# Longformer attention and a two-layer network on one core: another order of loads, copies and network units

## The chip, the core and the metric

The kernel runs on one core of one Trainium2 chip. The core has five engines that work side by side, each through its own list of instructions: PE (TensorE: matmuls and transposes), DVE (VectorE) and ACT (ScalarE) for elementwise work, POOL (GpSimd), which here issues casting DMAs and makes small copies, and SP (SyncE), which issues plain DMAs. PE writes its results to PSUM, which the kernel uses in eight banks; DVE and ACT read them from there.

The metric is device time in microseconds. Three runs of the kernel before took 411.75, 414.14 and 415.15 us; the median is 414.14.

## The reference

Two parts, one behind the other: attention with a band of 32 positions to each side and 8 global positions, for 8 batches of 8 heads (sequence 576, head size 64), and a network with a hidden layer of 2048 on its 4608 rows of 512.

```python
def _attn_ref(q, k, v, global_idx):
    B, H, S, D = q.shape                          # 8, 8, 576, 64
    scores = 1.0 / np.sqrt(D) * np.matmul(q, k.transpose(0, 1, 3, 2))
    pos = np.arange(S)
    mask = np.abs(pos[:, None] - pos[None, :]) <= 32
    is_global = np.zeros(S, dtype=bool)
    is_global[global_idx] = True
    mask = mask | is_global[:, None] | is_global[None, :]
    scores = np.where(mask, scores, -1000000000.0)
    attn = np.exp(scores - np.max(scores, axis=-1, keepdims=True))
    attn = attn / (np.sum(attn, axis=-1, keepdims=True) + 1e-09)
    return np.matmul(attn, v)

def _moe_ref(x, w_in, w_out):                     # (4608, 512), (512, 2048), (2048, 512)
    h = x @ w_in
    g = h * np.cos(h)
    return g @ w_out

def reference(**kw):
    y = _attn_ref(q, k, v, global_idx)
    x = y.transpose(0, 2, 1, 3).reshape(4608, 512)
    return _moe_ref(x, w_in, w_out)
```

All inputs and the output are float32. The kernel computes in float16 with float32 sums, and checks on the way whether the values allow that; if not, a general path at the end computes everything again.

## The kernel before

**Pairs and stages.** Two heads make a pair; there are 32 pairs, four to a batch. A stage s has two pairs, 2s and 2s + 1, and there are 16 stages. A pair's queries are cut into 11 blocks of 56. For each block a `kw` tile holds 8 global and 120 neighbouring keys and a `qb` tile holds the queries of both heads with the 8 global queries. The steps of a pair are:
- `local_k`, `local_q` and `globals_k`, `globals_q` fill `kw` and `qb`. The local part of pairs 0 to 7 comes from `kn` and `qn`, loaded in rows and turned by PE (`turned`); that of pairs 8 and up from `kT` and `qT`, which a transposing DMA has made, by a copy on DVE (lines 415 and 428). The first 8 columns are copied by POOL from `kgT` and `qgT` (lines 392, 396, 397).
- `scores`: the matmuls `st`, in three groups, an exponential on ACT and a product with the mask on DVE (`pm`).
- `values`: the matmuls `pv` of `pm` with the v rows `vw`, whose last column gives the sums, and the division on DVE (`xn`).
- `turn_x`: PE transposes `xn` (`tx`), and DVE copies it into `xT`, the transposed input of the network. At a batch's last pair POOL copies the eight global rows into their places (line 489).

**The network** takes 512 rows of x, a tile, at a time; there are 9. An input unit (`mlp_in`) makes 128 of the 2048 hidden columns of a tile: four matmuls `ph`, a cosine on ACT, a product on DVE (`g`). An output unit (`mlp_out`) is four matmuls `po`; four output units make 128 rows of the output, which DVE or ACT copies out of PSUM. So there are 144 units of each kind.

**Order.** Everything is written out by hand. The string `FRONT` lists the steps of stages 0 and 1 and the loads beside them. The string `ORDER` lists a stage's steps from stage 2 on, in which a, z are the stage's pairs, c, d those of the next stage, s scores, p values, x `turn_x`, k and q `kw` and `qb`, n the squares of `xn` for the check, 1 an input unit and 2 an output unit. A unit that isn't ready is left out at that place: an input unit needs its tile's x, an output unit all 16 input units of its tile. What then remains is the tail, 32 rounds of one input and one output unit and a last tile of outputs.

**Queues.** POOL issues the loads that change the type: `kn` and `qn` (line 258), `w_in` in four parts (639), `w_out` in one (655), the gathers of the global rows, and `cast_half`, which writes v, k and q in float16 to DRAM (lines 247 and 251), one call for four heads. SP issues what reads these float16 copies, the v rows `vw` (306 to 314, runs of 128 bytes), `vg` and the transposes, and the outputs. A `dma_start` on POOL stands in line with POOL's copies.

**PSUM.** Tag "s" has three banks (scores, turns, `tx`), "h" two (`ph`), "o" one (`po`), and `pv` two.

**The check.** `x_squares` sums the squares of `xn`; `weight_squares` squares a quarter of `w_in` on ACT, and `weight_norms` sums it with four matmuls `pn`; both run in stages 2 to 5. `finish_check` joins the sums on DVE and ends with a matmul `pt` and a flag; it stands in the fifth round of the tail.

## Time and profile before

| | |
|---|---|
| median of three runs | 414.14 us |
| the profiled execution's own time | 415.52 us |
| span of its profile | 413.8 us |
| granted TensorE clock, mean | 0.981 |
| PE busy | 332.7 us (80%), 2,678 instructions |
| PE's weight loads busy | 175.7 us (42%) |
| DVE busy | 269.9 us (65%) |
| ACT busy | 240.1 us (58%) |
| POOL busy | 109.2 us (26%) |
| SP's DMA queue, q1 | 27.89 MB, 54.4% of 16 engines |
| POOL's DMA queue, q0 | 18.75 MB, 44.3% of 16 engines |

PE has most of the busy time, and its transfers of weights run beside its matmuls. The busy shares are means over a front, fourteen stages and a tail, which differ. In the rows of the timeline that follow, the columns are the start and the duration in us, the engine, the line, the operation with what it writes and reads, and the shape; in brackets is the idle time before it and what ended it. In the rows of waits the numbers are the sum of the idle time, how many times, and the longest. In the groups they are busy us and the mean of one in ns, then the idle time before them.

### The profile page before, as it was taken

How to read it: one execution, taken by the hardware profiler on the slowest of the kernel's cores; microseconds unless marked ns; L12 is line 12 of the kernel's file. 1: busy time of each engine (PE TensorE's matmuls, PEld its weight loads, DVE VectorE, ACT ScalarE, POOL GpSimd, SP SyncE). 2: the span in 40 equal slices, each digit the busy share in tenths (PEclk: the TensorE clock that was granted, in tenths of full speed). 3: DMA queues.
4: the chain of work that ended last, by engine and by line, in shares of the span. 5: the costliest groups of instructions: out<-in, count | busy, mean ns of one | idle time of the engine just before them, and what ended most of it. 6: DMA issues, size and time to landing. Idle time of an engine off the chain costs nothing.

```text
span 413.8 us, 7344 instructions
## 1 busy us (share of the span) xinstructions
PE 332.7 (80%) x2678; PEld 175.7 (42%) x2678; DVE 269.9 (65%) x600; ACT 240.1 (58%) x351; POOL 109.2 (26%) x236
## 2 busy tenths in 40 slices
PE   0372218787778889997998899799999997999994
PEld 0162206443334445553554455354555542444441
DVE  7645117677568687887888887978888754434410
ACT  2571017888466767774768486667769662444310
POOL 6582004905740290047006400700310010000000
PEclk9999999989989999998999999999999998999999
DMA  6999999999999799999996999999591000101021
GB/s 88 122 169 198 216 150 85 152 135 121 152 114 166 62 135 157 170 107 168 174 118 113 156 191 96 138 136 148 83 119 53 26 27 27 51 27 51 25 78 57
DMA packets 188504, 47.18 MB, mean 114 GB/s; under 512 B 177005, under 2 KB 183405, under 8 KB 188205
## 3 DMA queue, kind: packets, MB, share of 16 engines
q1 hardware_dynamic: 124509, 27.89, 54.4%
q0 software_dynamic: 63952, 18.75, 44.3%
q8 instruction: 23, 0.38, 0.4%
q14 instruction: 20, 0.16, 0.2%
HBM read 47.73 MB, written 21.23 MB: 167 GB/s over the span
## 4 chain that ended last, share of the span: by engine, by line
PE 60%; DVE 8%; ACT 8%; POOL 7%; SPq 6%; issue 5%; DMA 4%; POOLq 0%; ACTq 0%
PE ph L497 27%; PE po L511 24%; PE pv L458 4%; SPq L314 3%; PE st L446 3%; DMA qn<-in_q_dram 2%; SPq L306 2%; ACT cos L500 2%; DVE o L518 2%; PE tx L481 2%; DVE g L501 2%; ACT sq L530 2%; ACT e L448 2%; POOL q L251 2%; DMA vw<-vg 2%
## 5 line engine op out<-in xcount | busy, mean ns | idle before, releaser
L511 PE MATMUL po<-w_out,g 128*128 128x512 f16 x576 | 145.5, 383 | 8.6 <-DVE o L518 8.6
L497 PE MATMUL ph<-xT,w_in 128*128 128x512 f16 x576 | 142.6, 387 | 6.7 <-DVE g L501 6.5
L500 ACT ACTIVATE cos<-ph,pio 128x512 f16<-128x512 f32 x144 | 97.2, 687 | 76.0 <-PE ph L497 75.7
L501 DVE TENSOR_TENSOR g<-cos,ph 128x512 f16<-128x512 f16 x144 | 96.5, 687 | 61.8 <-ACT cos L500 61.1
L511 PEld LDWEIGHTS <-g 128*128 128x128 f16 x576 | 55.7, 98 | 70.7 <-issue 12.1
L497 PEld LDWEIGHTS <-w_in 128*128 128x128 f16 x576 | 54.2, 99 | 69.1 <-issue 12.4
L448 ACT ACTIVATE e<-st 128x512 f16<-128x512 f32 (+1 forms) x96 | 49.4, 562 | 35.2 <-PE st L446 19.2
L489 POOL COPY xT<-xg 128x4 f16 x64 | 13.4, 210 | 199.0 <-DVE xT L484 195.4
L449 DVE TENSOR_TENSOR pm<-e,mask 128x512 f16<-128x512 f16 (+1 forms) x96 | 37.0, 408 | 27.8 <-ACT e L448 25.9
L446 PE MATMUL st<-qb,kw 128*128 128x128 f16 x352 | 33.6, 237 | 9.5 <-POOL kw L392 6.3
L458 PE MATMUL pv<-vw,pm 128*64 128x65 f16 x704 | 20.7, 207 | 22.9 <-DMA vw<-vg 22.8
L446 PEld LDWEIGHTS <-kw 128*128 128x128 f16 x352 | 26.8, 107 | 24.2 <-POOL kw L392 7.7
L469 DVE TENSOR_TENSOR xn<-pv,r_all 128x768 f16<-128x768 f32 x32 | 30.7, 958 | 1.1
L412 ACT COPY kw<-t 128x1320 f16<-128x1320 f16 x8 | 10.1, 1259 | 35.6 <-PE t L405 35.6
L458 PEld LDWEIGHTS <-pm 128*64 128x64 f16 x704 | 16.7, 120 | 26.9 <-DMA vw<-vg 13.5
L251 POOL DMA_DIRECT2D q<-in_q_dram x12 | 27.2, 2265 | 0.0
L530 ACT ACTIVATE sq<-xn 128x1536 f16<-128x1536 f16 x16 | 23.6, 1475 | 0.0
L415 DVE COPY kw<-kT 128x1320 f16<-128x1320 f16 x24 | 22.3, 929 | 0.0
L428 DVE COPY qb<-qT 64x616 f16<-64x616 f16 x48 | 22.1, 459 | 0.3
L481 PE MATMUL tx<-ident,xn 128*128 128x128 f16 x192 | 17.5, 232 | 5.6 <-DVE xn L469 4.8
L251 POOL DMA_DIRECT2D k<-in_k_dram x12 | 20.7, 1729 | 0.2
L463 DVE TENSOR_REDUCE dg<-pv 8x2 f32<-8x12 f32 x32 | 4.8, 151 | 24.4 <-PE pv L458 21.7
(105 smaller groups left out, 249.6 us busy)
## 6 DMA issues: line engine op xcount, KB each, us to landing
out_dram<-o SPq DMA_DIRECT2D x36, 256.0 KB
vw<-v SPq DMA_DIRECT2D x47, 165.0 KB
v<-in_v_dram POOLq DMA_DIRECT2D x16, 288.0 KB
k<-in_k_dram POOLq DMA_DIRECT2D x12, 288.0 KB
q<-in_q_dram POOLq DMA_DIRECT2D x12, 288.0 KB
vw<-v SPq DMA_DIRECT2D x16, 135.0 KB
w_in<-in_moe_w_in_dram POOLq DMA_DIRECT2D x4, 512.0 KB
w_out<-in_moe_w_out_dram POOLq DMA_DIRECT2D x1, 2048.0 KB
```

Source lines behind the costliest of these rows:

```text
L251: nc.gpsimd.dma_start(dst[s].rearrange("t (h d) -> t h d", h=4), dview(src, base, (D, S), (S * D, 4), (1, D)))
L446: nc.tensor.matmul(st[:, j], kp[:, g0 + j], view(qp[:, g0 + j], (1, P)), start=True, stop=True)
L448: nc.scalar.activation(e[:, :n], st[:, :n], AF.Exp, scale=scale)
L449: nc.vector.tensor_tensor(view(pm[:, g0], (1, n * P)), view(e, (1, n * P)), view(mask[:, g0], (1, n * P)), ALU.mult)
L458: nc.tensor.matmul(pv[r0 : r0 + C, j // 6, c0 : c0 + 65], pm[:, j, h], vp[:, j, h], start=True, stop=True)
L469: nc.vector.tensor_tensor(view(xn, (384, 2), (D, 6), (1, D)), view(pv, (512, 2), (65, 6), (1, D)), view(rp, (6, 2), (1, 6), (0, D)), ALU.mult)
L481: nc.tensor.transpose(tx[:, n], xn[:, n], ident16)
L497: nc.tensor.matmul(ph, w_in16[:, j, f * P : (f + 1) * P], xT[:, j, t * TT : (t + 1) * TT], start=(j == 0), stop=(j == NC - 1))
L500: nc.scalar.activation(cos, ph, AF.Sin, bias=pio2)
L501: nc.vector.tensor_tensor(g16[:, f], cos, ph, ALU.mult)
L511: nc.tensor.matmul(po, g16[:, f, s * P : (s + 1) * P], w_out16[:, f], start=(f == 0), stop=(f == NF - 1))
L530: nc.scalar.activation(sq, view(xn, (1, 2 * BP * P)), AF.Square, accum_out=x_sq[:, s : s + 1])
```

## The change

It moves work and adds one small copy; what is computed stays.

1. **Globals.** `globals_k` and `globals_q` are taken out of the steps k and q. For pairs 8 and up they stand at the start of the stage before theirs; for pairs 0 to 3 before the front's steps; for pairs 4 to 7 in `FRONT` as steps g.
2. **Casts.** All casts from half 4 on go into one function `casts`, called at a new step G, behind the second `values` of a stage. It begins with a copy of one element of `xn` on POOL, `gate`, which waits for that `xn`; behind it on POOL stand v, k and q of one half (in stage 4 of two halves, 6 and 7, and the gathers).
3. **Weights.** `w_out` moves from the end of `FRONT` to the start of stage 2. The four parts of `w_in` stand at other places in `FRONT`.
4. **The check.** The four `weight_squares` and `weight_norms` move from stages 2 to 5 to the tail, three rounds apart. `finish_check` is split: its DVE part stands in round 15 of the tail, the matmul and the flag in round 31 (`raise_flag`).
5. **Order of the units.** `ORDER` and `FRONT` are new, and stage 2 has a string of its own, `THIRD`, without output units. An output unit may now start before its tile's inputs are complete: the n-th four hidden parts need only be seven, in the tail twelve, units past their start. How many output units may be out by a stage is held by `outs_by`: none in stage 2, 4 in stage 3, 8 in stage 4, then 8 more with each stage. An input unit may be at most one tile ahead of the outputs. The tail is one loop over input and output units.
6. **PSUM.** In the front, `turned` uses the two banks of "h" and `turn_x` the one of "o", which the network doesn't use yet.

```diff
-ORDER = "sa0 sa1 sa2 2 2 sz0 2 sz1 2 sz2 pa 1 1 2 xa pz 1 1 2 xz n 1 1 kc qc 2 1 1 kd qd 2"
+ORDER = "sa0 sa1 sa2 2 2 2 sz0 2 sz1 sz2 pa 1 1 2 xa pz G 1 1 2 xz n 1 1 2 kc qc 1 kd qd 2 1"
+THIRD = "sa0 sa1 sa2 sz0 sz1 sz2 1 1 pa 1 1 xa pz G 1 1 kc qc xz 1 1 kd qd 1 n 1"
-FRONT = ("W0 k2 s0.0 s0.1 s0.2 q2 s1.0 s1.1 s1.2 k3 q3 L2 p0 s2.0 s2.1 s2.2 c2 W1 x0 p1 s3.0 s3.1 s3.2 p2 x1 "
-         "k4 q4 L3 v4 v5 W2 W3 c3 p3 x2 k5 q5 I O x3 n0 v6 v7")
+FRONT = ("s0.0 s0.1 s0.2 s1.0 s1.1 s1.2 k2 q2 g4 L2 p0 k3 q3 s2.0 s2.1 s2.2 g5 W0 c2 p1 x0 g6 W1 s3.0 s3.1 s3.2 g7 I "
+         "p2 x1 L3 v4 v5 p3 x2 k4 q4 x3 W2 k5 q5 n0 W3 c3 v6 v7")
...
-        t = ps.tile([P, RW, n], FP16, tag="s", bufs=3)
+        t = ps.tile([P, RW, n], FP16, tag="h" if front[0] else "s", bufs=2 if front[0] else 3)
...
-        tx = ps.tile([P, BP, P], FP16, tag="s", bufs=3)
+        tx = ps.tile([P, BP, P], FP16, tag="o" if front[0] else "s", bufs=1 if front[0] else 3)
...
+        return tot, onesf
+
+    def raise_flag(count):
+        tot, onesf = count
         pt = ps.tile([P, 512], FP32, tag="h", bufs=2)
...
-            if ins_q and ins_q[0][0] < ready[0]:
+            if ins_q and ins_q[0][0] < ready[0] and ins_q[0][0] < outs_q[0][0] + 2:
...
-            if outs_q and (outs_q[0][0] + 1) * NF <= ready[1]:
+            t, u = outs_q[0] if outs_q else (NTT, 0)
+
+            need = min(t * NF + 4 * (u % 4) + 12, NTT * NF) if tail[0] else min(t * NF + 4 * (u % 4) + 7, (t + 1) * NF)
+            if outs_q and need <= ready[1] and (tail[0] or NTT * NF - len(outs_q) < outs_by[0]):
                 mlp_out(*outs_q.pop(0))
...
+        def casts(s):
+
+            nc.gpsimd.tensor_copy(gate, xn_of[s][0:1, 1, 0, 0:1])
+            for n in range(4, 2 * B):
+                if s == (n - 2 if n < 7 else n - 3):
+                    cast_half(n, "vkq")
+            if s == 4:
+                for src, dst in ((k, kg32), (q, qg32), (v, vg32)):
+                    gather(src, dst, 1)
...
-        cast_half(4, "kq")
         for s in range(2, B * NP // 2):
-            if s < B * NP // 2 - 2:
-                cast_half(s + 2, "v")
-            if HY <= s + 3 < B * NP // 2:
-                cast_half(s + 3, "kq")
-            if s == 4:
-                for src, dst in ((k, kg32), (q, qg32), (v, vg32)):
-                    gather(src, dst, 1)
-            for step in ORDER.split():
+            if s == 2:
+                nc.gpsimd.dma_start(w_out16, moe_w_out.rearrange("(c p) n -> p c n", p=P))
+            outs_by[0] = 4 * (s - 2) if s < 5 else 8 * (s - 3)
+            for pr in (2 * s + 2, 2 * s + 3):
+                if 8 <= pr < B * NP:
+                    globals_kq(pr)
+            for step in (THIRD if s == 2 else ORDER).split():
...
                     x_squares(s - 1)
-                    if s < 6:
-                        weight_squares(s - 2)
+                elif step == "G":
+                    casts(s)
...
-            if s < 6:
-                weight_norms(s - 2)
         x_squares(B * NP // 2 - 1)
         tail[0] = True
-        for i in range(2 * NF):
+        for i in range(NTT * NF):
             one()
             two()
-            if i == 4:
-                finish_check()
-        two(NF)
+            if i in (3, 6, 9, 12):
+                weight_norms(i // 3 - 1)
+            if i in (0, 3, 6, 9):
+                weight_squares(i // 3)
+            if i == 14:
+                count = finish_check()
+            if i == 30:
+                raise_flag(count)
```

Three places show how this moves instructions. The first is POOL's list in the front; before, this stands in it (kn and qn are the loads of a half, v a cast, kw and qb the globals' copies of a pair):

```order
L258 DMA kn_86<-in_k_dram 72x4x512
L258 DMA qn_88<-in_q_dram 72x4x512
L247 DMA v_81<-in_v_dram 16x9216
L639 DMA w_in_113<-in_moe_w_in_dram 128x4x512
L392 COPY kw_94<-kgT 128x11x8
L396 COPY qb_98<-qgT 64x11x8
L397 COPY qb_98<-qgT 64x11x8
L258 DMA kn_87<-in_k_dram 72x4x512
L258 DMA qn_89<-in_q_dram 72x4x512
L639 DMA w_in_113<-in_moe_w_in_dram 128x4x512 x2
L247 DMA v_81<-in_v_dram 16x9216
```

Now, from the same loads of kn and qn on:

```order
L260 DMA kn_86<-in_k_dram 72x4x512
L260 DMA qn_88<-in_q_dram 72x4x512
L394 COPY kw_95<-kgT 128x11x8
L398 COPY qb_99<-qgT 64x11x8
L399 COPY qb_99<-qgT 64x11x8
L641 DMA w_in_113<-in_moe_w_in_dram 128x4x512
L249 DMA v_81<-in_v_dram 16x9216
L394 COPY kw_96<-kgT 128x11x8
L398 COPY qb_100<-qgT 64x11x8
L399 COPY qb_100<-qgT 64x11x8
L641 DMA w_in_113<-in_moe_w_in_dram 128x4x512
L394 COPY kw_97<-kgT 128x11x8
```

The globals of pairs 5, 6 and 7 now stand between the loads of the front. They write tiles that pairs 1, 2 and 3 have used, so the loads behind them on POOL come after the scores of those pairs.

The second place is POOL's list in a late stage; before:

```order
L392 COPY kw_94<-kgT 128x11x8
L396 COPY qb_98<-qgT 64x11x8
L397 COPY qb_98<-qgT 64x11x8
L392 COPY kw_95<-kgT 128x11x8
L396 COPY qb_99<-qgT 64x11x8
L397 COPY qb_99<-qgT 64x11x8
L247 DMA v_81<-in_v_dram 16x9216
L251 DMA k_80<-in_k_dram 2304x1x64
L251 DMA q_79<-in_q_dram 2304x1x64
L392 COPY kw_96<-kgT 128x11x8
L396 COPY qb_100<-qgT 64x11x8
L397 COPY qb_100<-qgT 64x11x8
```

Now:

```order
L662 COPY gate<-xn 1x1
L249 DMA v_81<-in_v_dram 16x9216
L253 DMA k_80<-in_k_dram 2304x1x64
L253 DMA q_79<-in_q_dram 2304x1x64
L394 COPY kw_94<-kgT 128x11x8
L398 COPY qb_98<-qgT 64x11x8
L399 COPY qb_98<-qgT 64x11x8
L394 COPY kw_95<-kgT 128x11x8
L398 COPY qb_99<-qgT 64x11x8
L399 COPY qb_99<-qgT 64x11x8
L662 COPY gate<-xn 1x1
L249 DMA v_81<-in_v_dram 16x9216
```

The casts stood at a stage's start, ahead of the globals of the next stage. They now follow the gate in the stage's second half, and the globals stand behind them, at the next stage's start, a stage ahead of their use.

The third place is ACT's list where the tail begins; before (sq is the check's last square of xn, cos an input unit, o a finished output block):

```order
L530 ACTIVATE sq,x_sq<-xn 128x1536
L500 ACTIVATE cos<-ph,pio_71 128x512 x7
L516 COPY o<-po 128x512
L500 ACTIVATE cos<-ph,pio_71 128x512 x8
L516 COPY o<-po 128x512
```

Now, with wsq a square of a quarter of the weights:

```order
L524 ACTIVATE sq,x_sq<-xn 128x1536
L494 ACTIVATE cos<-ph,pio_71 128x512
L531 ACTIVATE wsq<-w_in_113 128x2048
L494 ACTIVATE cos<-ph,pio_71 128x512 x3
L531 ACTIVATE wsq<-w_in_113 128x2048
L494 ACTIVATE cos<-ph,pio_71 128x512 x3
L531 ACTIVATE wsq<-w_in_113 128x2048
L494 ACTIVATE cos<-ph,pio_71 128x512 x3
L531 ACTIVATE wsq<-w_in_113 128x2048
L494 ACTIVATE cos<-ph,pio_71 128x512 x2
L510 COPY o<-po 128x512
```

The four squares now stand between the first input units of the tail, and the first block of outputs that ACT copies stands behind twelve of them.

More of the change, by code (lines that the diff above doesn't have):

```diff
@@ L428, in local_q @@
                 nc.vector.tensor_copy(to, view(qT[pr // 2 % 2][hp, pr % 2], (QB, NB), (1, QB)))
-    def copy_k(pr):
-        globals_k(pr)
-        local_k(pr)
-    def copy_q(pr):
-        globals_q(pr)
-        local_q(pr)
     def scores(pr, g):
@@ L583, in two @@
         for _ in range(n):
-            if outs_q and (outs_q[0][0] + 1) * NF <= ready[1]:
+            t, u = outs_q[0] if outs_q else (NTT, 0)
+            need = min(t * NF + 4 * (u % 4) + 12, NTT * NF) if tail[0] else min(t * NF + 4 * (u % 4) + 7, (t + 1) * NF)
+            if outs_q and need <= ready[1] and (tail[0] or NTT * NF - len(outs_q) < outs_by[0]):
                 mlp_out(*outs_q.pop(0))
+    outs_by = [0]
     ready = [0, 0]
-    tail = [False]
-    STEPS = {"k": copy_k, "q": copy_q, "s": scores, "p": values, "x": turn_x}
+    tail, front = [False], [True]
+    STEPS = {"s": scores, "p": values, "x": turn_x}
     with tc.manual_schedule():
@@ L626 @@
             nc.vector.memset(qb[i], 0.0)
-        for pr in (0, 1):
+        for pr in range(4):
+            if pr > 1:
+                load_v(pr)
             load_vg(pr)
@@ L630 @@
             globals_q(pr)
-        for pr in (2, 3):
-            load_v(pr)
-            load_vg(pr)
         pv = ps.tile([P, 2, 512], FP32, tag="pv", bufs=1)
@@ L652, in load_idx, with globals_kq @@
                 for g in range(G))
-        OTHER = {"L": load_qk, "W": load_w_in, "c": lambda s: cast_half(s, "v"), "v": load_values, "n": x_squares,
-                 "I": load_idx, "O": lambda _: nc.gpsimd.dma_start(w_out16, moe_w_out.rearrange("(c p) n -> p c n", p=P))}
+        def globals_kq(pr):
+            globals_k(pr)
+            globals_q(pr)
+        def casts(s):
[6 more added lines that the diff above has]
+                    gather(src, dst, 1)
+        gate = keep.tile([1, 1], FP16)
+        LOCAL = {"k": local_k, "q": local_q}
+        OTHER = LOCAL | {"g": globals_kq, "L": load_qk, "W": load_w_in, "c": lambda s: cast_half(s, "v"), "v": load_values, "n": x_squares,
+                 "I": load_idx}
         for step in FRONT.split():
@@ L658 @@
             f(*[int(x) for x in (step[1:] or "0").split(".")])
-        ready[0] = 1
+        ready[0], front[0] = 1, False
         for i in range(2):
@@ L681 @@
                     x_squares(s - 1)
-                    if s < 6:
-                        weight_squares(s - 2)
+                elif step == "G":
+                    casts(s)
                 else:
-                    f, pr = STEPS[step[0]], 2 * s + "azcd".index(step[1])
+                    f, pr = (STEPS | LOCAL)[step[0]], 2 * s + "azcd".index(step[1])
                     if pr < B * NP:
@@ L695 @@
                 build_globals(1)
-            if s < 6:
-                weight_norms(s - 2)
         x_squares(B * NP // 2 - 1)
         tail[0] = True
-        for i in range(2 * NF):
+        for i in range(NTT * NF):
             one()
             two()
-            if i == 4:
-                finish_check()
-        two(NF)
+            if i in (3, 6, 9, 12):
[6 more added lines that the diff above has]
+                raise_flag(count)
+        assert not outs_q
     es.close()
```

## The prediction
> **What bounds the kernel now.** I read the page first, for the span and the 40 slices of TensorE (PE) and of the DMA engines.
>
> ```profile
> span 413.8 us, 7344 instructions
> PE   0372218787778889997998899799999997999994
> DMA  6999999999999799999996999999591000101021
> ```
>
> A slice is 10.3 us. PE is near full from about slice 10 on and mostly empty in the first six, while the DMA engines are busy from the second slice to about 300 us. So PE sets the end, and what can be won are its gaps. The waits name them.
>
> ```profile
> PE pv L458 <- DMA vw<-vg: 22.8, 3, 13.0
> PE po L511 <- DVE o L518: 8.6, 12, 1.4
> PE st L446 <- POOL kw L392: 6.3, 3, 2.2
> PE pt L567 <- DVE onesf L565: 2.7, 1, 2.7
> ```
>
> PE waits 22.8 us for v rows, 8.6 us for an output bank to be copied out (0.7 us in each of twelve stages), 6.3 us for POOL and 2.7 us in the tail. The timeline of PE's rows gives the milestones.
>
> ```profile
> 48.30 0.26 PE L458 MATMUL pv<-vw,pm 128*64 128x65 f16 x1 [13.00 <-DMA vw<-vg]
> 61.09 1.14 PE L458 MATMUL pv<-vw,pm 128*64 128x65 f16 x22 [9.07 <-DMA vw<-vg]
> 65.65 0.63 PE L446 MATMUL st<-qb,kw 128*128 128x128 f16 x4
> 84.20 0.61 PE L446 MATMUL st<-qb,kw 128*128 128x128 f16 x8
> 103.16 0.78 PE L446 MATMUL st<-qb,kw 128*128 128x128 f16 x11
> 128.15 0.78 PE L446 MATMUL st<-qb,kw 128*128 128x128 f16 x11
> 149.58 0.78 PE L446 MATMUL st<-qb,kw 128*128 128x128 f16 x11
> 167.32 0.78 PE L446 MATMUL st<-qb,kw 128*128 128x128 f16 x11
> 335.04 1.03 PE L497 MATMUL ph<-xT,w_in 128*128 128x512 f16 x4
> ```
>
> The rows at 48.30 and 61.09 are the products of pairs 2 and 3 with their v rows. The front ends at 65.65, where stage 2 starts; stages 3 to 6 start at 84.20, 103.16, 128.15 and 149.58. A stage that nothing disturbs takes 167.32 - 149.58 = 17.74 us. The tail begins at about 335.0 and lasts 78.8 us.
>
> **The front: the loads that leave the way of the v rows.** Here are the queues by window. First 30 to 35 us (q0 is POOL's queue, q1 SP's, which loads vw; packets, then MB), then q1 alone in 60 to 65 us, then both in 232 to 236 us, a time of casts.
>
> ```profile
> q0 software_dynamic: 690, 0.89, 102.0%
> q1 hardware_dynamic: 633, 0.08, 21.2%
> ...
> q1 hardware_dynamic: 2864, 0.36, 101.6%
> ...
> q0 software_dynamic: 2459, 0.48, 138.2%
> q1 hardware_dynamic: 1957, 0.25, 78.9%
> ```
>
> ```profile
> 25.37 4.61 SPq L309 DMA_DIRECT2D vw<-v  x2
> 29.84 1.54 POOL L639 DMA_DIRECT2D w_in<-in_moe_w_in_dram  x2
> 38.32 1.20 POOL L655 DMA_DIRECT2D w_out<-in_moe_w_out_dram  x1 [5.09 <-issue]
> ...
> vw<-v SPq DMA_DIRECT2D x47, 165.0 KB
> w_in<-in_moe_w_in_dram POOLq DMA_DIRECT2D x4, 512.0 KB
> w_out<-in_moe_w_out_dram POOLq DMA_DIRECT2D x1, 2048.0 KB
> kn<-in_k_dram POOLq DMA_DIRECT2D x4, 288.0 KB
> ```
>
> Beside weights SP's loads get 633 / 5 = 127 packets per us; alone 573. A load of 165 KB in runs of 128 B is 1,320 packets, and pairs 2 and 3 need four, with their small vg rows about 5,500. They are issued from 25 us and end at 61. Between 21 and 40 us POOL issues four w_in loads, two kn/qn sets (0.59 MB each), two v casts and w_out: 2.1 + 1.2 + 0.6 + 2.1 = 6.0 MB.
>
> In the change, what is queued on POOL before 40 us is one kn/qn set, two w_in loads and one v cast, 1.9 MB: the globals of later pairs, which wait for a pair's scores, stand between them, and w_out, the other two w_in loads and the last v cast come behind the eight xT copies of x3. At 0.89 / 5 = 0.18 MB per us these 1.9 MB take 10.5 us. In that time q1 moves 1,330 packets; the other 4,200 take 7.3 us alone. So pair 3's v rows land near 25 + 10.5 + 7.3 = 43 instead of 61, and with the 4.6 us from 61.09 to 65.65 stage 2 starts near 48: **-18 us**. The extra PSUM tags ("h" for the turns, "o" for tx) only allow this: I find no wait of the front on a bank above 1 us, so by themselves 0 to -1.
>
> Then the bill. The 3.4 MB held back (two w_in, a v cast, w_out) are issued at about 50, after x3 and the xT copies, and take 3.4 / 0.18 = 19 us, to 69. Behind them on SP's queue stand vw of pairs 6 and 7, on POOL's the gated casts of half 4. From the v cast's landing near 58 to 69 q1 moves 11 x 127 = 1,400 packets, and the other 4,100 go at 1957 / 4 = 489 per us, to 77. Stage 2 loses a weight square and its four matmuls (1.9 us of ACT, 0.9 of PE, rows below) from the 18.55 between 65.65 and 84.20: 17, so stage 3 starts at 65 and would want pair 7 nine us later, at 74. It waits 3; its first output unit also waits for w_out, about 2 more. Stage 4 starts near 87 (before 103.16), and stage 5, 24.99 us later in the original, here some 22 later: four output units fewer and no norm, but the casts of halves 6 and 7 and six gathers now follow one another on POOL, and the DVE copies of kw and qb fall among them (below), 2 to 4 us. **Stage 5 starts near 109 instead of 128.15: -19.** Bounds: 98, if the held-back loads hide altogether (48 + 17 + 16 + 17); 121, if each of stages 3 to 5 waits another 4 us.
>
> At this point a rule of the Trainium skill speaks against the change. "DMA: Bandwidth & Descriptors", section "Queues, rings and completion order", says that a DMA engine serves its queues in turn, a packet from each. By this rule w_out's large rows slow SP's small ones wherever w_out stands. The trace agrees: 690 packets against 633.
>
> **Eleven full stages, 5 to 15.** They take 335.04 - 128.15 = 206.9 us, 18.8 each. The row of PE's wait on POOL, and what led to it, in one such stage and, last two rows, in the next, clean one:
>
> ```profile
> 224.75 2.84 DVE L415 COPY kw<-kT 128x1320 f16<-128x1320 f16 x1
> 225.05 2.19 POOL L251 DMA_DIRECT2D q<-in_q_dram  x1
> 228.55 0.38 PE L446 MATMUL st<-qb,kw 128*128 128x128 f16 x4 [2.07 <-POOL kw L392]
> ...
> 244.71 0.53 DVE L415 COPY kw<-kT 128x1320 f16<-128x1320 f16 x1
> 248.50 1.02 PE L511 MATMUL po<-w_out,g 128*128 128x512 f16 x4 [0.66 <-DVE o L518]
> ```
>
> Two things end here. POOL's k and q casts, queued ahead of the next stage's globals, hold PE, and while they issue, DVE's copy of kw takes 2.84 us instead of 0.53. In the change the globals of the next stage stand at a stage's start and the casts behind the gate, after the stage's last xn. A gate costs POOL a copy of one element, which I put at 0.3 us (no row of before shows one); behind it wait the casts, the xT copies and the next globals, all wanted 5 us later or more. DVE's order after xn is two g, the xT copies, two g, then kw and qb. I estimate that work at 5 us (a g like a cos, 0.69 in the rows of the tail, and PE's units between) and the casts at 4 (2.19 for q in the row, k no longer), so the copies mostly come after them. And the new ORDER puts scores between the last matmul of an output block and the first of the next, so the 0.66 us goes. A stage is then 17.74 - 0.66 = 17.1; I take 17.4, for the order brings PE close to DVE's pace. 11 x 17.4 = 191.4: **-15.5**. Bounds: 17.1 (-18.8) and 18.0 (-8.9).
>
> Can the DMA engines follow? In the clean stage they did, with the same casts, v rows and outputs, in 17.74 us; 0.3 less is asked of them.
>
> **The tail.** What leaves it and what comes:
>
> ```profile
> 342.81 1.03 PE L511 MATMUL po<-w_out,g 128*128 128x512 f16 x4
> 346.66 1.39 PE L497 MATMUL ph<-xT,w_in 128*128 128x512 f16 x4
> 350.95 1.03 PE L511 MATMUL po<-w_out,g 128*128 128x512 f16 x4
> 394.11 13.98 PE L511 MATMUL po<-w_out,g 128*128 128x512 f16 x64
> ...
> L537 ACT ACTIVATE wsq<-w_in 128x2048 f16<-128x2048 f16 x4 | 7.6, 1898 | 0.0
> L543 PE MATMUL pn<-wsq,ones 128*128 128x512 f16 x16 | 4.1, 378 | 0.5 <-DVE g L501 0.5
> L500 ACT ACTIVATE cos<-ph,pio 128x512 f16<-128x512 f32 x144 | 97.2, 687 | 76.0 <-PE ph L497 75.7
> ```
>
> A unit of four matmuls takes 13.98 / 16 = 0.87 us. From 342.81 to 350.95 four units run in 8.14 us instead of 3.5: the check's wait and the slow matmuls behind it cost 4.7. With its flag matmul sixteen steps after its DVE part, this is hidden behind output units: -4.7. The sixteen norm matmuls come in: +3.5, four units' time, all PE (their row has 4.1 beside other waits). The new rule of two() lets input units run ahead alone, eight or so; with two banks each waits for the cos (0.69) and the g (put at the same) of the one before the last, and 0.3 for handing over, an estimate: (0.87 + 0.69 + 0.69 + 0.3) / 2 = 1.27 instead of 0.87, +3.2. Of the four 1.9 us squares on ACT some 2 us show. Sum **+4** (from -1, all hidden, to +8, every square shown).
>
> **Sum.** 109 + 191.4 + 78.8 + 4 = 383 of span. The profiled execution's 415.52 stands 1.4 above the median 414.14, which is within 0.4 of the span 413.8; I go by the median: **384**.
>
> **Rivals.** *The loads are only postponed.* The v rows of pairs 6 to 11 each meet w_out or the late casts; stages 3 to 5 keep their old length, stage 5 starts at 121: 396. For: 127 packets per us beside weights. Against: w_out lasts about 12 us of a 17 us stage.
> *The bill never shows.* Stage 5 at 98, the rest as summed: 373. For: q1 has a stage's lead.
> *Slower: the lock of the casts.* If DVE reaches kw and qb before the q cast is issued, each of stages 3 to 15 pays as at 224.75, where the two copies of the casts cost 2.3 us, and with four copies and POOL's xT copies up to twice that, 4.5. Stage length 17.4 + 4.5 = 21.9: 11 x 21.9 = 241, stage 5 at 118: 118 + 241 + 82.8 = 442. At 2.3 it is 109 + 217 + 83 = 409. It turns slower than before from about 2.7 us per stage. For: casts were in the way of three stages and are now in all. Against: the 5 us of DVE work ahead. The Trainium skill, "SBUF — State Buffer", section "SBUF: two separate sides", has this as an exclusive lock between GpSimd and certain DVE operations; the row at 224.75 agrees.
> *It does not do what it says.* Another queue holds the front (the v casts, half 1), gain 5, and stages 18.3: 407 to 412.
>
> **Chances.** Forecast 0.50; postponed 0.20; bill never shown 0.16; does not do it 0.07; lock 0.07. Range 370 to 404: it takes in the forecast, most of the hidden bill and the postponed loads, some 0.82. The three runs of before spread from 411.75 to 415.15, so 1% is about what can be told. Faster by over 1% (under 410): 0.88; within 1%: 0.06; slower: 0.06.
>
> **What would show it.** Pair 3's product near 43 and stage 2's first scores near 48; q1's packets per us above 400 before 45; no PE wait on POOL kw and none on o of 0.66; L415 at 0.53 from stage 5 on; stage starts 17.4 apart; a pt matmul without wait; a tail of about 83 us. I am wrong if pv waits for vw again in stages 2 and 3 for over 8 us, or if L415 stays long in every stage.

## The result, and the profile after

The changed kernel takes 396.06 us (median of four runs, 395.26 to 397.13); the kernel before took 414.38 beside it (411.75 to 415.15). The ratio is 0.957, with a 95% interval from 0.952 to 0.962. The forecast was 384, with a range of 370 to 404: faster as forecast, by 18 us where 30 were forecast. Of the kernels with the early cast and with the old order, further down, one execution each, the profiled one, ran in a slower state of the chip (394.99 and 407.23 us): it is left out of their times (with it the medians are 390.21 and 400.55), and its rows are read for what lies between them, not for where they stand.

The profiled execution took 397.13 us. Its page, with the 40 slices of PE, of PE's granted clock and of the DMA engines:

```profile
span 395.4 us, 7373 instructions
PE   0272179576778889899999999999999979999993
PEclk9997558969999999999999999999999999999999
DMA  6989979999999999999999999999990000010121
```

A slice is 9.9 us now. The front is still empty, and the DMA engines are still full from the second slice to about 300 us. New in the record is a clock of 0.5 in the fifth and sixth slice. The rows don't show PE slower there than before, though the record of the kernel before has 1.00: six transposes `tx` take 0.82 us at 62.17 before the change and 0.82 at 50.51 after it, against 0.50 to 0.51 later on in both. The waits of PE after the change (sum, times, longest):

```profile
PE pv L452 <- issue: 10.3, 2, 9.4
PE pv L452 <- DMA vw<-vg: 8.5, 4, 5.1
...
PE pv L452 <- DMA vw<-v: 4.2, 2, 3.0
...
PE po L505 <- DMA w_out<-in_moe_w_out_dram: 3.6, 1, 3.6
...
PE po L505 <- DVE o L512: 1.3, 1, 1.3
...
PE st L440 <- POOL qb L399: 1.0, 1, 1.0
```

The wait for v rows is still 23 us (10.3 + 8.5 + 4.2; the 9.4 called issue stands ahead of pair 2's product, which reads v rows). There is a new one for w_out, 3.6. The wait for POOL fell from 6.3 to 1.0 and the one for o from 8.6 to 1.3. The milestones in PE's timeline:

```profile
49.81 0.77 PE L452 MATMUL pv<-vw,pm 128*64 128x65 f16 x21 [1.20 <-DMA vw<-v]
...
55.47 1.35 PE L440 MATMUL st<-qb,kw 128*128 128x128 f16 x11
...
74.98 0.78 PE L440 MATMUL st<-qb,kw 128*128 128x128 f16 x11
79.32 1.49 PE L505 MATMUL po<-w_out,g 128*128 128x512 f16 x4 [3.57 <-DMA w_out<-in_moe_w_out_dram]
...
83.50 1.02 PE L452 MATMUL pv<-vw,pm 128*64 128x65 f16 x22 [1.52 <-DMA vw<-vg]
...
91.61 0.76 PE L452 MATMUL pv<-vw,pm 128*64 128x65 f16 x22 [3.03 <-DMA vw<-v]
...
99.68 0.77 PE L440 MATMUL st<-qb,kw 128*128 128x128 f16 x11 [0.95 <-POOL xT L483]
...
118.22 0.77 PE L440 MATMUL st<-qb,kw 128*128 128x128 f16 x11 [0.76 <-issue]
...
140.05 0.81 PE L440 MATMUL st<-qb,kw 128*128 128x128 f16 x11
...
192.29 0.78 PE L440 MATMUL st<-qb,kw 128*128 128x128 f16 x11
...
209.20 0.78 PE L440 MATMUL st<-qb,kw 128*128 128x128 f16 x11
...
309.84 1.89 PE L491 MATMUL ph<-xT,w_in 128*128 128x512 f16 x8
```

| | before | after | difference |
|---|---|---|---|
| stage 2 starts | 65.65 | 55.47 | -10.2 |
| stage 3 starts | 84.20 | 74.98 | -9.2 |
| stage 4 starts | 103.16 | 99.68 | -3.5 |
| stage 5 starts | 128.15 | 118.22 | -9.9 |
| the tail starts | 335.04 | 309.84 | -25.2 |
| the span ends | 413.8 | 395.4 | -18.4 |

So the front's 10 us are mostly gone at stage 4: stage 3 takes 24.7 us, with 8.1 us of waits for loads. Stage 4, 24.99 before, takes 18.54; what shortened it is not taken apart here. The eleven stages from 5 on take 191.6 instead of 206.9, and a clean one 209.20 - 192.29 = 16.91 instead of 17.74. The tail takes 85.6 instead of 78.8.

DVE's copies of kw, by group; before the change, then after it:

```profile
L415 DVE COPY kw<-kT 128x1320 f16<-128x1320 f16 x24 | 22.3, 929 | 0.0
```

```profile
L417 DVE COPY kw<-kT 128x1320 f16<-128x1320 f16 x24 | 13.3, 556 | 0.0
```

No copy takes 2.8 us any more; the longest is 0.96.

### The profile page after: what moved, and what is told of

The parts are those of the page before. It is cut to its first block, busy times and chain, and to the rows that moved or that the text cites. A ratio compares the mean times of both kernels' runs of the same rounds, so it can differ in the third digit from the quotient of the medians.

```text
span 395.4 us, 7373 instructions
## 1 busy us (share of the span) xinstructions
PE 328.3 (83%) x2678; PEld 174.7 (44%) x2678; DVE 260.6 (66%) x600; ACT 238.8 (60%) x351; POOL 114.8 (29%) x250
## 4 chain that ended last, share of the span: by engine, by line
PE 67%; DMA 10%; DVE 8%; ACT 5%; issue 3%; SPq 3%; another core or an unknown queue 1%; POOL 0%; ACTq 0%; DVEq 0%
PE po L505 28%; PE ph L491 27%; DMA q<-in_q_dram 4%; PE st L440 4%; PE pv L452 4%; DMA vw<-vg 3%; DMA vw<-v 3%; DVE g L495 2%; PE tx L475 2%; SPq L308 2%; ACT cos L494 2%; DVE xn L463 1%; PE t L407 1%; ACT sq L524 1%
## 5 line engine op out<-in xcount | busy, mean ns | idle before, releaser
L505 PE MATMUL po<-w_out,g 128*128 128x512 f16 x576 | 140.4, 380 | 5.0 <-DMA w_out<-in_moe_w_out_dram 3.6
L442 ACT ACTIVATE e<-st 128x512 f16<-128x512 f32 (+1 forms) x96 | 47.6, 561 | 14.3 <-PE st L440 9.3
L662 POOL COPY gate<-xn 1x1 f16<-1x1 f16 x14 | 2.5, 182 | 143.3 <-DVE xn L463 143.3
L452 PE MATMUL pv<-vw,pm 128*64 128x65 f16 x704 | 20.6, 204 | 23.1 <-issue 10.3
L440 PE MATMUL st<-qb,kw 128*128 128x128 f16 x352 | 30.8, 238 | 4.2 <-ACT e L442 1.5
L483 POOL COPY xT<-xg 128x4 f16 x64 | 20.5, 320 | 22.0 <-DVE xT L478 18.6
L510 ACT COPY o<-po 128x512 f32<-128x512 f32 x18 | 10.5, 586 | 22.4 <-PE po L505 21.9
L512 DVE COPY o<-po 128x512 f32<-128x512 f32 x18 | 12.3, 685 | 12.1 <-PE po L505 12.0
```

Source lines behind the costliest of these rows:

```text
L440: nc.tensor.matmul(st[:, j], kp[:, g0 + j], view(qp[:, g0 + j], (1, P)), start=True, stop=True)
L442: nc.scalar.activation(e[:, :n], st[:, :n], AF.Exp, scale=scale)
L452: nc.tensor.matmul(pv[r0 : r0 + C, j // 6, c0 : c0 + 65], pm[:, j, h], vp[:, j, h], start=True, stop=True)
L505: nc.tensor.matmul(po, g16[:, f, s * P : (s + 1) * P], w_out16[:, f], start=(f == 0), stop=(f == NF - 1))
```

## Experiments

The theory at this point: the late stages gain by the gate and the early globals; the front's loads are only postponed, since the DMA queues are full up to stage 4. The rival: the order of the loads makes the front's gain, and the order of the units that of the late stages. Each kernel but the last two is the changed one with one edit, and the kernel before, run beside them, took 412.1 to 413.3 us. The changed kernel was not run again beside them, so the ratios to the kernel before (0.957 for the changed kernel) tell more than differences in us; 0.01 is 4 us.

### The loads of the front

All loads back at the places of the kernel before:

```diff
-FRONT = ("s0.0 ... g5 W0 c2 p1 x0 g6 W1 s3.0 s3.1 s3.2 g7 I "
-         "p2 x1 L3 v4 v5 p3 x2 k4 q4 x3 W2 k5 q5 n0 W3 c3 v6 v7")
+FRONT = ("W0 s0.0 ... g5 c2 W1 p1 x0 g6 s3.0 s3.1 s3.2 g7 I "
+         "p2 x1 L3 v4 v5 W2 W3 c3 p3 x2 k4 q4 O x3 k5 q5 n0 v6 v7")
...
-            if s == 2:
-                nc.gpsimd.dma_start(w_out16, ...)
```

> The changed kernel with all five loads of the front's POOL list (four parts of w_in, the v cast of half 3, w_out) put back where they stood among the steps of the kernel before; the globals stay where the change put them. Theory 1, as predicted: these bytes take the DMA engines from pair 3's v rows. Then pair 3's product, at 49.8 in the changed kernel and 61.1 in the one before, lies at 56 to 60, stage 2 starts at 61 to 65 instead of 55.5, stage 3 has no wait for v rows and w_out, and the time is 396 to 402. Theory 2, the front moves a fixed number of packets and any order gives the same start of stage 4: stage 4 starts at 95 to 100 and the time is 391 to 396, like the runs with w_out (394.1) or the v cast (390.2) moved alone.

394.07 us, ratio 0.955 (0.948 to 0.962): no slower than the changed kernel. Its rows of PE:

```profile
55.06 0.23 PE L452 MATMUL pv<-vw,pm 128*64 128x65 f16 x1 [11.32 <-DMA vw<-vg]
56.19 0.81 PE L452 MATMUL pv<-vw,pm 128*64 128x65 f16 x21 [0.89 <-DMA vw<-vg]
...
98.38 0.77 PE L440 MATMUL st<-qb,kw 128*128 128x128 f16 x11 [0.98 <-POOL xT L483]
```

Both theories are right on what they describe. The mechanism of the front is there: with the weights ahead of them, pair 3's rows come at 56.19 instead of 49.81, and stage 2 starts at 61.88. But stage 3 then waits for no load, and stage 4 starts at 98.4, as in the changed kernel (99.7). **All in all the new order of the loads moves the wait from the front to stage 3 and brings nothing by stage 4.** But this run moves the v cast of half 3 along with the weights, and that cast is worth some 5 us when it alone stands early (below): what the late weights bring, the late v cast takes back. With w_out alone back in the front it is the same:

```diff
-         "p2 x1 L3 v4 v5 p3 x2 k4 q4 x3 W2 k5 q5 n0 W3 c3 v6 v7")
+         "p2 x1 L3 v4 v5 p3 x2 k4 q4 O x3 W2 k5 q5 n0 W3 c3 v6 v7")
```

> The changed kernel with one edit: the load of w_out is issued ahead of the xT turn of pair 3, near 40 us, as before the change, instead of at the start of stage 2 (60.3). Theory 1, taking w_out out of the way of pair 3's v rows is what brought the front's gain: these rows, which land at 49.8, land near 56, stage 2 starts near 61 instead of 55.5; the wait for w_out in stage 3 (3.6 us) goes; the time is 398 to 401. Theory 2, w_out's place only chooses which wait shows: stage 4 starts within 1 us of 99.7 and the time is 395 to 397.

394.07 us, ratio 0.956 (0.950 to 0.962). Pair 3's rows come at 52.2 instead of the 56 expected, stage 2 starts at 57.9, and stage 4 at 94.8, 5 us earlier than theory 2 had it; the time is the same all the same, for stages 5 and 6 then take 20.5 and 20.7 us. The Trainium skill ("DMA: Bandwidth & Descriptors", section "Queues, rings and completion order") has it that a DMA engine serves its queues in turn, a packet from each. What the prediction drew from that, that w_out slows the small rows wherever it stands, fits these two runs: pair 3's rows come 2.4 us later with w_out ahead of them, and 6.4 with all the weights.

To test the bound itself, half of the weights' bytes are left out:

```diff
-        x3 W2 k5 q5 n0 W3 c3 v6 v7
+        x3 k5 q5 n0 c3 v6 v7
...
-            nc.tensor.matmul(ph, w_in16[:, j, f * P : (f + 1) * P], ...
+            nc.tensor.matmul(ph, w_in16[:, j, f % 8 * P : (f % 8 + 1) * P], ...
...
-            nc.tensor.matmul(po, g16[...], w_out16[:, f], ...
+            nc.tensor.matmul(po, g16[...], w_out16[:, f % 8], ...
...
-                nc.gpsimd.dma_start(w_out16, ...)
+                nc.gpsimd.dma_start(w_out16[:, 0:8], ...)
```

> The changed kernel with half of the weights' bytes: two of the four parts of w_in are loaded and 1 MB of w_out, and the units use the loaded half twice, so the output is another; every instruction of PE, DVE and ACT stays. Theory 1, up to stage 4 the kernel is bound by what the two DMA queues can move, so that an order of the loads shifts waits and not their sum: 2 MB less at the 0.19 MB per us that POOL's queue moves there is 10 us less in the way, the waits for w_out and v rows in stage 3 (8 us) go, stage 4 starts near 91 instead of 99.7, and the time is 387 to 390. Theory 2, the v rows alone and the engines set it: stage 4 starts at 97 or later, the time is 393 or more.

389.66 us, ratio 0.944 (0.939 to 0.948); the output is another. Stage 4's first scores in this run:

```profile
93.72 0.77 PE L440 MATMUL st<-qb,kw 128*128 128x128 f16 x11 [0.95 <-POOL xT L483]
```

6.0 us earlier and 6.4 us in all: stage 3 waits for bytes. Theory 1 has the time right and the start too early: it is less than the 10 us that the bytes take, for stage 3 then takes 18.0 us, near its own work. The sum of the bytes isn't the whole bound either: with all of them, and w_out early, stage 4 starts at 94.8.

Which bytes can come earlier at no cost? In the changed kernel SP's queue all but stops from 55 to 60 us, and from 60 to 70 it has no row. Its packets from 55 to 60, then a window of PE (length, busy time, clock, share of the DMA engines, GB/s), then the rows of POOL's timeline, then of SP's:

```profile
q1 hardware_dynamic: 59, 0.01, 1.5%
```

```profile
52.00:60.00 8.00, 5.83 (x80) 0.50 0.46 34
```

```profile
55.51 2.05 POOL L483 COPY xT<-xg 128x4 f16 x8 [15.52 <-DVE xT L478]
57.67 1.55 POOL L641 DMA_DIRECT2D w_in<-in_moe_w_in_dram  x2
59.20 0.55 POOL L249 DMA_DIRECT2D v<-in_v_dram  x1
```

```profile
52.62 1.49 SPq L316 DMA_DIRECT2D vw<-vg  x2
67.82 3.89 SPq L311 DMA_DIRECT2D vw<-v  x2
```

The v cast of half 3, from which pairs 6 and 7 are loaded, stands on POOL behind the xT copies, which wait 15.5 us for pair 3. SP can go on only at 67.82. POOL's other loads stand there too, so from 52 to 60 us the DMA engines move little at all: 34 GB/s, and 197 in the 8 us behind it. So this cast alone was moved ahead:

```diff
-         "p2 x1 L3 v4 v5 p3 x2 k4 q4 x3 W2 k5 q5 n0 W3 c3 v6 v7")
+         "p2 x1 L3 c3 v4 v5 p3 x2 k4 q4 x3 W2 k5 q5 n0 W3 v6 v7")
```

> The changed kernel (396.1 us, 0.957 of before) with one edit: the v cast of half 3 (pairs 6 and 7) stands ahead of the v loads of pair 4 in the front's string, so POOL issues it near 40 us instead of 59.2. In the changed kernel SP's queue has 59 packets between 55 and 60 us and none from 60 to 70. Theory 1, the late cast leaves that queue idle and so makes the rows of pairs 6 and 7 late: those rows land before 72, the two waits of PE for v rows in stage 3 (1.5 and 3.0 us) go, stage 2 starts at most 2 us later since the cast now shares with pair 3's rows, and the time falls by 3 to 5 us, to about 392. Theory 2, the bytes are only postponed and some load is late whatever the order: pair 3's rows land 3 us later, or w_out does, and the time stays within 1 us of 396.

388.93 us, ratio 0.944 (0.938 to 0.950): **5 us faster than the changed kernel by the ratios, 7 by the times**, a little more than theory 1 said. Stage 3 takes 95.27 - 78.42 = 16.9 us instead of 24.7 and waits for no v rows (2.6 us for w_out stay), and SP's queue moves 2,609 packets from 56 to 60 us. In its profiled execution stage 2 starts at 58.80, 3.3 later, where theory 1 allowed 2. The loss was a queue that stood idle for one cast. It also shows what the late weights are worth: with the v cast early, the kernel takes 388.93 us with the weights late and 394.07 with them at their old places (the v cast's own place differs a little between the two). So moving the weights was worth some 5 us, and the v cast that was moved with them hid it.

### The late stages: gate and globals

The casts at the start of the stage, ahead of the globals, without the gate:

```diff
         for s in range(2, B * NP // 2):
...
+            casts(s)
             for pr in (2 * s + 2, 2 * s + 3):
                 if 8 <= pr < B * NP:
                     globals_kq(pr)
...
         def casts(s):
-            nc.gpsimd.tensor_copy(gate, xn_of[s][0:1, 1, 0, 0:1])
...
                 elif step == "G":
-                    casts(s)
+                    pass
```

> The changed kernel with the casts at the start of the stage, ahead of the globals, without the gate; order, loads and tail stay. Theory 1, what held PE before the change was that the globals stood behind the casts in the stage that needs them; as they now stand a stage ahead, the place of the casts does not matter: late stages stay at 16.9 to 17.2, the time at 395 to 399. Theory 2, the gate keeps the casts off DVE's copies and products: DVE rows beside a cast take 2 to 3 us more, three or more stages grow by 2 us as at 224.75 in the kernel before, the time is 402 or more.

413.60 us, ratio 1.002 (0.999 to 1.006). **Without the gate the whole gain is gone**, and stages 8 to 11 take 18.3 to 20.1 us. Theory 2 has the time; its mechanism is only a part. DVE's 24 copies of kw take 22.3 us in all again. What stands on DVE, POOL and PE around one late stage:

```profile
217.41 0.53 DVE L417 COPY kw<-kT 128x1320 f16<-128x1320 f16 x1
219.42 2.15 DVE L417 COPY kw<-kT 128x1320 f16<-128x1320 f16 x1
...
238.38 0.95 DVE L430 COPY qb<-qT 64x616 f16<-64x616 f16 x2 [3.38 <-DMA qT<-q]
```

```profile
217.96 1.64 POOL L253 DMA_DIRECT2D k<-in_k_dram  x1
219.03 2.18 POOL L253 DMA_DIRECT2D q<-in_q_dram  x1
...
223.40 1.64 POOL L253 DMA_DIRECT2D k<-in_k_dram  x1
224.47 2.18 POOL L253 DMA_DIRECT2D q<-in_q_dram  x1
```

```profile
219.34 0.78 PE L440 MATMUL st<-qb,kw 128*128 128x128 f16 x11
...
239.43 0.80 PE L440 MATMUL st<-qb,kw 128*128 128x128 f16 x6 [2.87 <-issue]
```

Two things come back. POOL, held by nothing, issues a cast in the last microseconds of a stage, where DVE copies kw: five of the 24 copies take 2.15 to 3.35 us. This is what the prediction called the lock. The Trainium skill, "SBUF — State Buffer", section "SBUF: two separate sides", calls the ports that GpSimd and certain DVE operations share an exclusive lock; these rows agree on the block, and show it on the side of DVE while POOL issues. And the casts of two stages go out within 10 us of one another, at 218 and 223; the transposes and v rows behind them come late: DVE waits 3.38 us for qT and PE 2.87 for DVE. With the gate the k casts stand 16.92 us apart, one stage, at 204.04 and 220.96. PE's waits of this kind past the front, and a longer one for o:

```profile
PE st L440 <- issue: 7.5, 5, 2.9
...
PE po L505 <- DVE o L512: 4.1, 1, 4.1
```

That is 11.6 us, 9.5 more than in the changed kernel, of the 17.5 in all; the rest is not taken apart further. **The late stages pay for the second thing, not for the lock**: the copy of 2.15 us at 219.42 costs PE 0.1 us, and the stage loses its 3 us ahead of 239.43, to qT. The lock costs in stage 4, where the wait for o of 4.1 us stands behind the copy of 3.35. That it is the pairing of the casts that makes the transposes late is read from these rows; no run tests it alone.

The other half: the globals back in the steps k and q, with the gate left.

```diff
-            for pr in (2 * s + 2, 2 * s + 3):
-                if 8 <= pr < B * NP:
-                    globals_kq(pr)
...
-        LOCAL = {"k": local_k, "q": local_q}
+        LOCAL = {"k": both_k, "q": both_q}    # globals, from pair 8 on, and the local part
```

> The changed kernel with the globals of pairs 8 and up back in the steps that fill kw and qb, behind the gated casts on POOL; all else stays. Theory 1, moving the globals a stage ahead is half of the late stages' gain: POOL ends the casts some 4 us behind the gate and then copies, PE waits for kw or qb by about 2 us in most stages, the time is 410 or more. Theory 2, the gate alone does it, since the casts end before the copies are wanted: late stages stay at 16.9 to 17.3, the time at 396 to 400.

416.87 us, ratio 1.010 (1.006 to 1.013). All of the gain is gone here too. PE's waits, then the row of the longest and what POOL waited for ahead of it:

```profile
PE st L440 <- POOL qb L399: 25.5, 6, 17.4
```

```profile
137.34 0.26 POOL L399 COPY qb<-qgT 64x88 f16<-64x88 f16 x1 [5.93 <-DMA vg<-in_v_dram,gidx_rows]
```

```profile
137.66 1.33 PE L440 MATMUL st<-qb,kw 128*128 128x128 f16 x11 [17.38 <-POOL qb L399]
```

17.4 of the 25.5 us stand ahead of stage 5: in stage 4 two halves of casts and six gathers lie between the gate and the globals. From there on it is 1.1 to 1.2 us ahead of stages 8, 10 and 12, where the xT copies stand in between too. So theory 1 is right in direction and result, but not by 2 us in most stages. The DVE copies stay short (13.5 us in all), as the gate has it. A gate puts the casts right ahead of the next stage, so the globals must no longer stand behind them. But nearly all of the price is the double cast and the gathers of stage 4: from stage 5 to the end this run takes 277.9 us and the changed kernel 277.1. What late globals cost with the gathers elsewhere was not run.

### Order, gathers, norms, banks

The old order of steps from stage 3 on:

```diff
-ORDER = "sa0 sa1 sa2 2 2 2 sz0 2 sz1 sz2 pa 1 1 2 xa pz G 1 1 2 xz n 1 1 2 kc qc 1 kd qd 2 1"
+ORDER = "sa0 sa1 sa2 2 2 sz0 2 sz1 2 sz2 pa 1 1 2 xa pz G 1 1 2 xz n 1 1 kc qc 2 1 1 kd qd 2"
```

> The changed kernel with the old order of steps from stage 3 on (the step G, the casts, put behind the second pair's values); globals, casts, loads and tail stay as changed. A late stage takes 16.92 us in the changed kernel and took 17.74 before, undisturbed. Theory 1, the order of the units brought this 0.8: a late stage takes 17.7 again and the time is 0.8 x 12 = 10 us longer, 405 to 406. Theory 2, it came from the globals and casts: a late stage stays below 17.1, the time at 396 to 398.

398.54 us, ratio 0.968 (0.960 to 0.976). Two starts of stages in it:

```profile
199.43 0.78 PE L440 MATMUL st<-qb,kw 128*128 128x128 f16 x11
...
216.84 0.78 PE L440 MATMUL st<-qb,kw 128*128 128x128 f16 x11
```

A clean stage takes 17.41 us, between the two theories: of the 0.83 between 17.74 and 16.91 the order brings 0.50. Stages 8 to 14 are clean in both kernels, so this makes 3.5 us; the time is 2.5 us longer by the medians and 4.6 by the ratios.

The gathers at the start of stage 3:

```diff
-            if s == 4:
-                for src, dst in ((k, kg32), (q, qg32), (v, vg32)):
-                    gather(src, dst, 1)
...
+            if s == 3:
+                for src, dst in ((k, kg32), (q, qg32), (v, vg32)):
+                    gather(src, dst, 1)
             for step in (THIRD if s == 2 else ORDER).split():
```

> The changed kernel with the six gathers of the second half's global rows issued at the start of stage 3, behind its globals, instead of behind the two halves of casts in stage 4. Stage 5 takes 21.8 us in the changed kernel, where a late stage takes 16.9. Theory 1, the gathers on POOL and in the DMA queue beside the double cast cause most of this: stage 5 takes 18 to 19 us, the time is 393. Theory 2, it is the build of the global columns and the double cast: stage 5 stays above 21 and the time within 1 us of 396.

394.20 us, ratio 0.952 (0.945 to 0.959), which can't be told from the changed kernel. Stage 5 takes 18.9 us, as theory 1 has it; but it takes 18.9 too in the runs with the old loads, with the old banks and with half of the weights, where the gathers stay. What made it 21.8 in the changed kernel's profile is left open.

The weight squares and norms back in stages 2 to 5:

```diff
                 elif step == "n":
                     x_squares(s - 1)
+                    if s < 6:
+                        weight_squares(s - 2)
...
+            if s < 6:
+                weight_norms(s - 2)
...
-            if i in (3, 6, 9, 12):
-                weight_norms(i // 3 - 1)
-            if i in (0, 3, 6, 9):
-                weight_squares(i // 3)
```

> The changed kernel with the four weight squares and norms back in stages 2 to 5. They cost 1.9 us of ACT and 0.9 us of PE each. Theory 1, as the prediction has it, in the tail they are paid for, in stages 2 to 5 they partly lie beside waits for DMA: the tail falls from 85.6 by 5 to 6 us, stages 2 to 5 grow by 1 to 4 in all, the time is 392 to 395. Theory 2, stages 2 to 5 pay in full, 1.9 us of ACT each: the time is 396 to 399.

392.56 us, ratio 0.949 (0.943 to 0.955): theory 1. The tail takes 390.9 - 312.9 = 78.0 instead of 85.6, and stages 2 to 5 together 89.1 instead of 84.6. The stages grow by 4.5, a little more than theory 1 allowed, and the tail falls by 7.6. So this part of the change costs some 3 us, at the edge of what can be told, since the intervals of the two ratios meet.

The banks of the front:

```diff
-        t = ps.tile([P, RW, n], FP16, tag="h" if front[0] else "s", bufs=2 if front[0] else 3)
+        t = ps.tile([P, RW, n], FP16, tag="s", bufs=3)
...
-        tx = ps.tile([P, BP, P], FP16, tag="o" if front[0] else "s", bufs=1 if front[0] else 3)
+        tx = ps.tile([P, BP, P], FP16, tag="s", bufs=3)
```

> The changed kernel with the turns and the tx of the front back in the three banks of tag s. Theory 1, as predicted, the banks only allow and bring nothing by themselves: 396 within 1 us, since the front waits for loads. Theory 2, with the loads moved the banks have become a wait: pair 3's scores come later, stage 2 starts 2 us or more after 55.5, the time is 398 or more.

395.56 us, ratio 0.958 (0.953 to 0.964): no effect, as predicted. Its stage 4 starts at 97.8 and its stage 6 at 135.2, against 99.7 and 140.1: so much do executions with the same loads differ there.

### A faster version, and the clock

Three edits together: the early v cast, the gathers in stage 3 (as above), the norms in stages 3 to 6 (`3 <= s < 7` and `s - 3` in the diff of the norms).

> The changed kernel with the v cast of half 3 early (390.2 alone), the gathers at the start of stage 3 (394.2 alone), and the weight squares and norms in stages 3 to 6 instead of the tail (392.6 alone in stages 2 to 5). If the gains lie in different places they add: 4 to 6 by the cast, 1 to 2 by the gathers, 3 to 4 by the norms, so 385 to 388. If the DMA queues still set stages 3 to 6, the gathers and the norms' place give nothing beside the cast: 389 to 391.

389.50 us, ratio 0.942 (0.937 to 0.946): it beats both kernels, and the early cast alone does so by as much (388.93). The gains do not add. The tail falls to 78.5, but stages 3 to 7, freed of waits by the cast, now show each square: input units wait for g by up to 2.35 us behind a square of ACT.

To this, matmuls that nothing reads were added where PE waits for v rows in the front:

```diff
-         "p2 x1 L3 c3 v4 v5 p3 x2 ...
+         "d30 p2 x1 L3 c3 v4 v5 d12 p3 x2 ...
...
+        def busy(n):
+            t = ps.tile([P, 512], FP32, tag="o", bufs=1, name="idle")
+            for _ in range(n):
+                nc.tensor.matmul(t, ident16, view(mask[:, 0], (1, 512)), start=True, stop=True)
```

> The kernel of the three moves with 42 matmuls of 512 columns that nothing reads, 30 ahead of pair 2's product and 12 ahead of pair 3's, where PE waits for v rows. In the changed kernel the granted clock is 0.50 from 36 to 60 us and a group of 11 score matmuls takes 1.35 us instead of 0.78 there. Theory 1, the clock falls because PE idles and the front pays for it: kept busy, PE runs at full clock from 45 to 63, stage 2 starts 2 to 3 us earlier, and the time falls by 1 to 3 us against the three moves. Theory 2, loads set the front and the slow matmuls lie beside them: stage 2 starts up to 2 us earlier and stage 4 does not, the time is the same within 1 us.

389.48 us, ratio 0.943 (0.938 to 0.948): the same time. Windows of PE in this run (length, PE's busy time, its clock, the DMA share, GB/s):

```profile
48.00:50.00 2.00, 0.75 (x24) 1.00 1.29 102
...
52.00:54.00 2.00, 1.85 (x35) 0.50 1.46 109
```

The clock stays at 1.00 up to pair 3's product, and stage 2 starts 2.0 us earlier than without, stage 4 1.6, which is less than such starts differ between executions. In the time nothing is left of it, as theory 2 has it. Theory 1 is not refuted in full: it wanted full clock up to 63, and from 52 to 60 us, where stage 2 begins, the clock was 0.50 all the same.

## Why the prediction was right or wrong

The range held the time, the direction was right, and the forecast was 12 us too low. By its own sum, of the span: 109 + 191.4 + 82.8 = 383 was forecast, and 118.2 + 191.6 + 85.6 = 395.4 measured.

- **The front, "-18": measured -10, and gone again by stage 4.** The step that failed is "stage 2 starts near 48". "What is queued on POOL before 40 us is one kn/qn set" was wrong: a second one was issued at 38.5, and is in neither the 1.9 nor the 3.4 MB of the sum. Beside them SP's queue did better than the 127 packets per us taken, 221 and 262 per us in the windows of 30 to 35 and 40 to 45 us:

```profile
q1 hardware_dynamic: 1107, 0.14, 27.3%
...
q1 hardware_dynamic: 1312, 0.16, 37.5%
```

  Pair 3's product came at 49.8 instead of 43, and from there to stage 2 it took 5.7 instead of 4.6 us. Its sign, "above 400 before 45", failed too. The run with the old loads shows that the cause named was real (56.2 against 49.8); its price was paid back in stage 3, by waits for w_out (3.6) and for the v rows behind the cast that was moved with the weights (4.5).
- **The bill, "stage 5 near 109": 118.2.** This is the term that was mis-sized, by 9. Stage 2 started 7.5 us late, and the forecast let stage 3 wait 3 + 2 us; it waited 8.1. The reason was seen only in part: the v cast of half 3 was put among the loads held back, but not that SP's queue would stand idle for some 12 us for it. The rival "the loads are only postponed" (396) names this mechanism and the time; its stage 5 at 121 counts 4 us of waits in stage 5 itself, which lie behind that start; without them it is 117, near the 118.2. "The bill never shows" is refuted.
- **Eleven stages, "17.4": 191.6 against 191.4, by offsetting errors.** A clean stage takes 16.91, below the bound of 17.1; stages 5 (21.8) and 7 (18.4) take the rest back, so that the sum holds is luck. That "two things end here" was right: the wait on POOL's globals and that on o are gone, and the copy of kw is short. The mis-sized term is the wait on o, "0.66". In the kernel before, four scores take 0.23 us from start to start with the bank free (151.92) and 1.05 with the wait (153.01):

```profile
151.92 0.39 PE L446 MATMUL st<-qb,kw 128*128 128x128 f16 x4
152.15 1.03 PE L511 MATMUL po<-w_out,g 128*128 128x512 f16 x4
153.01 0.39 PE L446 MATMUL st<-qb,kw 128*128 128x128 f16 x4
154.06 1.02 PE L511 MATMUL po<-w_out,g 128*128 128x512 f16 x4 [0.66 <-DVE o L518]
```

  So it cost 0.82, and 17.74 - 0.82 = 16.92. The price of the parts was not seen: all of the gain is gone when the gate or the early globals are taken away.
- **The lock, as a rival: refuted for this kernel, by a hair.** "DVE's order after xn" kept the copies behind the casts: none takes longer than 0.96 us. But the "5 us" of DVE work are 4.0 in a late stage (xn ends at 203.25, kw begins at 207.28), and the casts behind the gate, itself 0.18 us, end at 207.30. Without the gate some copies are blocked, as the rival says, but the late stages lose their time to late transposes; that 413.6 lies in the rival's range, 409 to 442, is chance.
- **The tail, "+4": +6.8.** The flag's wait fell from 2.7 to 0.5 us, as said. The windows show 132 and 193 matmuls of units in the tail instead of 128 and 189, another 1.7 us, which the sum had left out. With the norms' 3.5, 4.2 us of waits for g (1.35, 1.55, 0.64 and 0.63), where 3.2 + 2 were forecast, and 4.7 less for the check, 4.7 of the 6.8 are named. The two units come out of stage 15, which takes 16.05 us.
- **The banks, "0 to -1"**: 0, within what can be told.

Where the 18 us lie, by the starts of the stages: 3.5 by stage 4, 6.5 in stage 4, 15.3 in stages 5 to 15, and the tail gives 6.8 back. What each part is worth when it alone is undone: 17 to 19 us for the gate, some 21 for the early globals, most of it in stage 4, and 2.5 to 4.6 for the order of the units; the norms in the tail cost some 3, the late v cast 5 to 7. These don't add up, since they depend on one another.

## What to carry to other kernels

Where transfers bound a stretch, moving several out of the way at once can move the wait only; look for the queue that then stands idle, and leave early what it waits for. An instruction that issues transfers in an in-order queue is worth placing by what stands behind it as much as by what it collides with: hold it by a gate, and take what is needed soon out from behind it. Undo each part alone before crediting it: parts that need one another each seem to be worth the whole gain, and two that work against each other can seem to be worth nothing. Then look in the rows whether the time was lost where the theory said.

## What the hardware showed

- The clock of PE fell to 0.50 without one long idle time: in the last run it was 1.00 from 38 to 50 us and 0.50 from 52 to 60, and ahead of that PE idled 1.13, 0.33 and 1.02 us between 47.8 and 52.2 us, the last as it fell. In the changed kernel it was 0.50 from 36 to 60, and a group of 11 score matmuls took 1.35 us instead of 0.78. A group at 33.94 in the kernel before took 1.35 us too, where the record shows 1.00; so in the front the lengths of the rows tell more than the record. What the half clock costs here is not shown.
- A DVE copy of kw (128x1320) that meets the issue of k and q casts on POOL can take 2.15 to 3.35 us instead of 0.53, four to six times as long, while the cast's own issue rows keep their 1.64 and 2.18 us. Not each one does: copies of qb (64x616) beside the k cast keep 0.45 to 0.47, and a copy of kw at 118.76 in the changed kernel, inside the rows of two casts, took 0.53.
